# Sinkhorn-sorted attention and a gated MLP on one core: the copies of transposed q and k out of PSUM, with the stride moved from the written side to the read side

## The chip, the core and the metric

The kernel runs on one core of one Trainium2 chip. Its engines are TensorE (PE in the profile; its weight loads are PEld), VectorE (DVE), ScalarE (ACT), GpSimd (POOL) and the queue of SyncE (SP), which only issues DMAs here. Matmul results land in PSUM; DVE and ACT carry them from there to SBUF. The metric is the device time of one execution in microseconds.

## The reference

Four batches of eight heads, 768 tokens, head size 64. The tokens of a head form 8 blocks of 96. A matrix P (8 by 8 for each head, from `sort_net`, five Sinkhorn rounds) mixes the blocks of k and of v; each block of q then attends to the mixed block at its place. The result, 512 wide over all heads, goes through a gated MLP with a mixing over tokens.

```python
P = sort_net
for _ in range(5):
    P = np.exp(P - np.max(P, axis=-1, keepdims=True))
    P = P / (np.sum(P, axis=-1, keepdims=True) + 1e-09)
    P = P / (np.sum(P, axis=-2, keepdims=True) + 1e-09)
k_sorted = np.einsum('bhij,bhjcd->bhicd', P, k_b)     # v_sorted alike
attn = softmax(q_b @ k_sorted^T / sqrt(D))            # in each block of 96
x = (attn @ v_sorted), heads side by side             # 4 x 768 x 512
h = np.maximum(x @ w_in, 0.0)                         # 512 -> 1024
u, v = h[..., :512], h[..., 512:]
v_n = (v - mean(v)) / np.sqrt(var(v) + 1e-06)
v_s = np.einsum('ts,bsd->btd', w_spatial, v_n) + b_spatial[None, :, None]
return (u * v_s) @ w_out
```

## The kernel before

The work is cut into small units, functions whose names begin with `u_`. The order in which they are issued is written out by hand in a table (`ORDER`), one entry for each unit with its arguments; each engine runs its own instructions in that order, one after the other, and waits where an operand or a buffer isn't ready. In the table, batches overlap: while the MLP of one batch runs, the transposes and scores of the next are already issued. A PSUM tile (`ps0` to `ps3`, each two banks of 512 fp32 in all 128 partitions) is named in the entry, and so is the engine that copies it out (A for ACT, D for DVE). `G` is 6, `D` is 64, `n` is 64 or 128.

The loads (`u_L`, on POOL's queue) lay a head's 768 tokens so that partition p holds the tokens 6p to 6p+5: token 6x+g stands in partition x at place g. A transpose with 128 partitions as input thus gives the tokens of one g only, and six of them, one for each g, fill a PSUM tile in the order (g, x).

- `u_QT` transposes q of two heads (`hp`) by matmuls with the identity, g by g, and copies the PSUM tile to `qT` in SBUF, where the tokens stand in their natural order, 6x+g. With `ih` 0 or 1 it does half of the partitions (64, so 384 tokens), with 2 all of them (768 tokens).
- `u_KT` does the same for k, with the mixing matrix `pd` in the identity's place, so that transposing and mixing are one matmul (`mix_T`).
- `u_VM` mixes v in PSUM and copies it to `vm` in SBUF; `u_VC` then copies `vm` to `vb` (one block of 96 tokens in partitions 0 to 95) by eight DMAs for each batch on SP's queue.
- `u_SC` makes the scores of four blocks from `kT` and `qT`, and ACT's exponential writes them to `ex`. `u_AT` multiplies `ex` with `vb`; DVE divides by the sums (`rec`, then `x_sb`).
- `u_SK` is a Sinkhorn round: an exponential on ACT, then sums, reciprocals and products on DVE. The last writes `p_x`, from which `pd` is made. In the table the first four half transposes of q stand between these rounds.
- `u_XT`, `u_VP`, `u_LN`, `u_LA`, `u_UP`, `u_SP` and `u_OP` are the MLP: transposes of x, the two projections, normalisation, spatial mixing with the gate, the output projection and its DMA.

The copies go through one helper, so that in the profile all copies by ACT have line 104 and all by DVE line 106, and the tiles' names tell them apart:

```python
def copy(eng, out, in_):
    if eng == "A":
        nc.scalar.copy(out=out, in_=in_)
    else:
        nc.vector.tensor_copy(out=out, in_=in_)
```

In the profile they are CAST rows, `kT<-ps` and `qT<-ps`. The matmuls of `u_QT` have line 276, of `u_KT` 291, of `u_VM` 313, of `u_SC` 341, of `u_AT` 364, of `u_VP` 405, of `u_UP` 446, of `u_SP` 458, of `u_OP` 479.

Of the kernel before, what the change touches and what calls it, by code (L numbers as in the profile page):

```python
# [59 lines left out]
def kernel(  # L60
# [17 lines left out]
    G = S // 128  # L78
# [20 lines left out]
    def ps_tile(n, dt=FP32):  # L99
        return psum.tile([128, 2, 512 if dt == FP32 else 1024], dt, name=f"ps{n}", tag=f"ps{n}")  # L100
# [6 lines that stand above are left out]
# [153 lines left out]
    def q_tile(b, hp):  # L260
        if ("qT", b, hp) not in st:
            st["qT", b, hp] = att.tile([128, S], BF16, name="qT", tag="qT", bufs=5)
        return st["qT", b, hp]

    def k_tile(b, hp):
        if ("kT", b, hp) not in st:
            st["kT", b, hp] = att.tile([128, S], BF16, name="kT", tag="kT", bufs=5)
        return st["kT", b, hp]

    def u_QT(ps, eng, b, hp, ih):  # L270
        b, hp, ih = int(b), int(hp), int(ih)
        lo, n = (0, 128) if ih == 2 else (ih * 64, 64)
        t = ps_tile(ps).rearrange("p x c -> p (x c)")
        for g in range(G):
            for hh in range(2):
                nc.tensor.matmul(  # L276
                    t[hh * 64:hh * 64 + 64, g * n:(g + 1) * n],
                    lhsT=st["q", b][lo:lo + n, 2 * hp + hh, g * D:(g + 1) * D],
                    rhs=ident[lo:lo + n, lo:lo + n],
                    start=True, stop=True,  # L280
                )
        copy(
            eng,
            q_tile(b, hp)[:, lo * G:(lo + n) * G].rearrange("p (x g) -> p g x", g=G),
            t[:, 0:n * G].rearrange("p (g x) -> p g x", g=G),
        )

    def mix_T(t, src, b, hp, lo, n):
        for g in range(G):
            for hh in range(2):  # L290
                nc.tensor.matmul(  # L291
                    t[hh * 64:hh * 64 + 64, g * n:(g + 1) * n],
                    lhsT=src[:, 2 * hp + hh, g * D:(g + 1) * D],
                    rhs=pd[b][:, 2 * hp + hh, lo:lo + n],
                    start=True, stop=True,
                )

    def u_KT(ps, eng, b, hp, ih):
        b, hp, ih = int(b), int(hp), int(ih)
        lo, n = (0, 128) if ih == 2 else (ih * 64, 64)  # L300
        t = ps_tile(ps).rearrange("p x c -> p (x c)")
        mix_T(t, st["k", b], b, hp, lo, n)
        copy(
            eng,
            k_tile(b, hp)[:, lo * G:(lo + n) * G].rearrange("p (x g) -> p g x", g=G),
            t[:, 0:n * G].rearrange("p (g x) -> p g x", g=G),
        )

    def u_VM(ps, eng, b, hp):
# [217 lines left out]
```

## Time and profile before

| | |
|---|---|
| time, median of 3 runs | 216.38 us (215.75 to 216.55) |
| the profiled execution | 216.17 us, its span 214.0 us |
| busy: PE | 163.0 us (76%) |
| busy: DVE | 133.9 us (63%) |
| busy: ACT | 131.0 us (61%) |
| busy: POOL | 35.3 us (16%) |
| copies of kT and qT on ACT | 13 + 13, 31.8 + 29.4 us |
| copies of kT and qT on DVE | 7 + 7, 12.6 + 15.1 us |
| granted TensorE clock, mean | 0.904 |

Busy time is an average over stages with different limits, so the stages are read apart. The span runs from the first instruction to the last; the execution's time is 2.2 us longer. All times in the rows are microseconds from the span's start, unless they are marked ns. A row of a group has its count behind the x, then the busy time, the mean ns of one, and the engine's idle time just before such instructions with what ended it.

### The profile page before, as it was taken

The numbers are of one execution on the slowest core, as the hardware profiler recorded it, in microseconds if no ns is written. First come the engines' busy times: TensorE is split into PE (matmuls) and PEld (weight loads), VectorE is DVE, ScalarE is ACT, GpSimd is POOL, SyncE is SP. The second block draws the span as 40 slices with busy tenths as digits, with TensorE's granted clock in tenths as the row PEclk, the third lists the DMA queues.
The fourth block names the chain that finished last, engine by engine and source line by source line (L and its number), as shares of the span: only waits on it lengthen the run. The fifth ranks groups of instructions, "written<-read, shape, count | busy, mean of one in ns | idle before, by whom it ended". The sixth has DMA issues, their size and how long they took to land.

```text
span 214.0 us, 4057 instructions
## 1 busy us (share of the span) xinstructions
PE 163.0 (76%) x1716; PEld 101.0 (47%) x1728; DVE 133.9 (63%) x244; ACT 131.0 (61%) x133; POOL 35.3 (16%) x41
## 2 busy tenths in 40 slices
PE   0283856996438969959659996595999999999790
PEld 0241445954335545535424555273665566455330
DVE  3236689776685774524725857589968585664900
ACT  3180854669997699993693769939455524580031
POOL 7405906201300000003430000011000033002000
PEclk9997575599995995888997999999999999999999
DMA  5999999999995000350460042071001600024025
GB/s 93 192 203 206 211 223 236 204 204 204 211 245 93 0 2 3 54 100 0 47 100 3 14 182 101 0 121 35 0 3 39 254 4 0 3 105 189 0 103 193
DMA packets 21921, 22.38 MB, mean 105 GB/s; under 512 B 1040, under 2 KB 18704, under 8 KB 21904
## 3 DMA queue, kind: packets, MB, share of 16 engines
q0 software_dynamic: 14864, 12.19, 36.4%
q1 hardware_dynamic: 7040, 9.94, 16.2%
q8 instruction: 13, 0.21, 0.4%
q14 instruction: 4, 0.03, 0.0%
HBM read 24.78 MB, written 6.29 MB: 145 GB/s over the span
## 4 chain that ended last, share of the span: by engine, by line
PE 53%; ACT 25%; DVE 12%; DMA 5%; issue 3%; POOL 1%; ACTq 0%; DVEq 0%; POOLq 0%
PE ps L458 13%; ACT kT L104 11%; ACT qT L104 10%; PE ps L446 9%; PE ps L405 8%; PE ps L479 8%; DVE qT L106 4%; PE ps L364 4%; DMA q_in<-in_q_dram 4%; PE ps L341 3%; DVE kT L106 3%; PE ps L386 2%; PE ps L313 2%; PE ps L291 2%; ACT u_sb L110 1%
## 5 line engine op out<-in xcount | busy, mean ns | idle before, releaser
L104 ACT CAST kT<-ps 128x768 bf16<-128x768 f32 (+1 forms) x13 | 31.8, 2475 | 9.5 <-PE ps L291 9.5
L458 PE MATMUL ps<-wspT,v_sb 128*128 128x384 bf16 x192 | 34.9, 337 | 3.5 <-ACT kT L104 3.5
L349 ACT ACTIVATE ex<-ps 96x768 bf16<-96x768 f32 x32 | 24.9, 811 | 15.2 <-PE ps L341 15.1
L470 POOL TENSOR_TENSOR gt<-z,u_sb 128x768 bf16<-128x768 f32 x7 | 11.5, 1647 | 129.0 <-DVE z L464 101.1
L104 ACT CAST qT<-ps 128x768 bf16<-128x768 f32 (+1 forms) x13 | 29.4, 2394 | 5.4 <-PE ps L276 5.4
L405 PE MATMUL ps<-w_in_sb,xT 128*128 128x512 bf16 x88 | 24.6, 411 | 4.4 <-ACT kT L104 1.8
L458 PEld LDWEIGHTS <-v_sb 128*128 128x128 bf16 x192 | 18.7, 100 | 16.3 <-issue 5.4
L446 PE MATMUL ps<-xT,w_in_sb 128*128 128x384 bf16 x128 | 24.6, 338 | 0.7 <-ACT kT L104 0.7
L479 PE MATMUL ps<-w_out_sb,gt 128*128 128x512 bf16 x92 | 22.2, 380 | 1.8 <-DVE gt L470 1.7
L464 DVE TENSOR_TENSOR z<-ps,b_bc 128x768 f32<-128x768 f32 x16 | 15.3, 954 | 12.3 <-PE ps L458 12.3
L372 DVE TENSOR_TENSOR x_sb<-ps,rec 96x512 bf16<-96x512 f32 x32 | 22.0, 687 | 1.1
L104 ACT COPY o_sb<-ps 128x1024 f32<-128x1024 f32 x11 | 11.1, 1012 | 17.3 <-PE ps L479 15.9
L419 DVE BATCH_NORM_STATS2 stats<-v_sb 128x6 f32<-128x512 bf16 x24 | 16.3, 677 | 8.7 <-ACT v_sb L110 8.4
L110 ACT ACTIVATE u_sb<-ps 128x768 bf16<-128x768 f32 x16 | 13.0, 810 | 11.1 <-PE ps L446 10.9
L341 PE MATMUL ps<-qT,kT 64*96 64x96 bf16 x256 | 12.1, 232 | 9.1 <-ACT qT L104 4.8
L276 PE MATMUL ps<-ident,q_in 128*64 128x128 bf16 (+1 forms) x240 | 9.4, 233 | 10.8 <-DMA q_in<-in_q_dram 9.2
L364 PE MATMUL ps<-vb,ex 96*128 96x65 bf16 x256 | 14.2, 208 | 3.5 <-ACT qT L104 2.1
L106 DVE CAST qT<-ps 128x768 bf16<-128x768 f32 (+1 forms) x7 | 15.1, 2239 | 2.6 <-PE ps L276 2.6
L446 PEld LDWEIGHTS <-w_in_sb 128*128 128x128 bf16 x128 | 12.3, 100 | 9.2 <-issue 2.0
L341 PEld LDWEIGHTS <-kT 64*96 64x96 bf16 x256 | 9.7, 139 | 14.5 <-issue 12.7
L405 PEld LDWEIGHTS <-xT 128*128 128x128 bf16 x96 | 9.7, 107 | 14.2 <-issue 6.5
L364 PEld LDWEIGHTS <-ex 96*128 96x128 bf16 x256 | 12.7, 107 | 7.3 <-issue 4.2
(63 smaller groups left out, 203.9 us busy)
## 6 DMA issues: line engine op xcount, KB each, us to landing
out_dram<-o_sb SPq DMA_DIRECT2D x12, 512.0 KB, 2.8
vb<-vm SPq DMA_DIRECT2D x32, 99.0 KB, 4.6
v_in<-in_v_dram POOLq DMA_DIRECT2D x4, 768.0 KB, 13.5
k_in<-in_k_dram POOLq DMA_DIRECT2D x4, 768.0 KB, 15.9
q_in<-in_q_dram POOLq DMA_DIRECT2D x3, 768.0 KB, 20.5
wsp_nat<-in_moe_w_spatial_dram POOLq DMA_DIRECT2D x1, 1152.0 KB, 21.9
w_in_sb<-in_moe_w_in_dram POOLq DMA_DIRECT2D x2, 512.0 KB, 16.4
q_in<-in_q_dram POOLq DMA_DIRECT2D x2, 384.0 KB, 10.9
```

Source lines behind the costliest of these rows:

```text
L104: nc.scalar.copy(out=out, in_=in_)
L106: nc.vector.tensor_copy(out=out, in_=in_)
L341: nc.tensor.matmul(t[0:BLK, hh, ii * BLK:(ii + 1) * BLK], lhsT=kT[rows, i * BLK:(i + 1) * BLK], rhs=qT[rows, i * BLK:(i + 1) * BLK], start ...
L349: nc.scalar.activation(out=e[:, 0:2 * NI * BLK].rearrange("p (h c) -> p h c", h=2), in_=t[0:BLK, :, 0:NI * BLK], func=AF.Exp, scale=scale,)
L364: nc.tensor.matmul(t[:, hh, ii * VW:ii * VW + D + 1], lhsT=e[:, c:c + 128], rhs=vb[b % 2][:, ih * NI + ii, 2 * hp + hh, 0:D + 1], start=Tr ...
L372: nc.vector.tensor_mul(out=x_sb[:, :, hp * 128:hp * 128 + 128].rearrange("p i (h d) -> p h i d", h=2), in0=tv[:, :, :, 0:D], in1=_raw_ap(r ...
L405: nc.tensor.matmul(t[:, x, :], lhsT=st["xT", b][:, kc, n * 128:(n + 1) * 128], rhs=w_in_sb[:, kc, DH:DFF], start=(kc == 0), stop=(kc == KC ...
L419: nc.vector.bn_stats(out=stats, in_=v_sb[:, x, :])
L446: nc.tensor.matmul(t[:, x, 0:HW], lhsT=w_in_sb[:, kc, mc * 128:(mc + 1) * 128], rhs=st["xT", b][:, kc, ih * HW:(ih + 1) * HW], start=(kc = ...
L458: nc.tensor.matmul(t[:, x, 0:HW], lhsT=st["v_sb", b, n][:, mc * 128:(mc + 1) * 128], rhs=wspT[:, n, x * HW:(x + 1) * HW], start=(n == 0), ...
L464: nc.vector.tensor_add(out=z.rearrange("p (x c) -> p x c", x=2), in0=t[:, :, 0:HW], in1=b_bc.rearrange("p (x c) -> p x c", x=2),)
L479: nc.tensor.matmul(t[:, x, :], lhsT=st["gt", b, mc][:, c * 128:(c + 1) * 128], rhs=w_out_sb[:, mc, :], start=(mc == 0), stop=(mc == FC - 1),)
```

## The change

The copy's loops are put in another order. Before, it ran over g outside and x inside: PSUM was read one element after the other, and `qT` or `kT` was written with a step of G elements. Now it runs over x outside and g inside: the 384 or 768 elements in SBUF are written one after the other, and PSUM is read with a step of `n` fp32, six times, then from the next x. What is moved and where it ends up is the same. All instructions, their order on each engine and the DMAs are the same.

```diff
@@ u_QT
         copy(
             eng,
-            q_tile(b, hp)[:, lo * G:(lo + n) * G].rearrange("p (x g) -> p g x", g=G),
-            t[:, 0:n * G].rearrange("p (g x) -> p g x", g=G),
+            q_tile(b, hp)[:, lo * G:(lo + n) * G].rearrange("p (x g) -> p x g", g=G),
+            t[:, 0:n * G].rearrange("p (g x) -> p x g", g=G),
         )
@@ u_KT
         copy(
             eng,
-            k_tile(b, hp)[:, lo * G:(lo + n) * G].rearrange("p (x g) -> p g x", g=G),
-            t[:, 0:n * G].rearrange("p (g x) -> p g x", g=G),
+            k_tile(b, hp)[:, lo * G:(lo + n) * G].rearrange("p (x g) -> p x g", g=G),
+            t[:, 0:n * G].rearrange("p (g x) -> p x g", g=G),
         )
```

## The prediction

> **What bounds the kernel now.** I read the page's chain first, to see which engine the end hangs on, then the busy times by stage, then who TensorE (PE) waited for, and last the rows of the copies.
>
> ```profile
> PE 53%; ACT 25%; DVE 12%; DMA 5%; issue 3%; POOL 1%; ACTq 0%; DVEq 0%; POOLq 0%
> PE ps L458 13%; ACT kT L104 11%; ACT qT L104 10%; PE ps L446 9%; PE ps L405 8%; PE ps L479 8%; DVE qT L106 4%; PE ps L364 4%; DMA q_in<-in_q_dram 4%; PE ps L341 3%; DVE kT L106 3%; PE ps L386 2%; PE ps L313 2%; PE ps L291 2%; ACT u_sb L110 1%
> ```
>
> Over half of the chain is PE. The copies that the change touches (kT and qT, on ACT and DVE) are 11 + 10 + 4 + 3 = 28% of it, 60 of 214 us. That isn't what can be won: shortened, they hand the chain to PE. So the question is how long PE is idle, stage by stage (columns: length, PE busy, weight load, DVE, ACT, POOL, granted clock, DMA share, GB/s):
>
> ```profile
> 0.00:20.00 20.00, 7.54 (x76) 4.34 (x76) 7.62 (x38) 7.42 (x10) 8.34 (x17) 0.98 1.09 171
> 20.00:40.00 20.00, 14.10 (x250) 11.05 (x248) 16.93 (x23) 12.14 (x13) 11.61 (x14) 0.59 1.24 220
> 40.00:65.00 25.00, 16.91 (x246) 12.75 (x246) 18.23 (x26) 21.43 (x17) 2.92 (x3) 0.91 1.29 215
> 65.00:160.00 95.00, 77.94 (x816) 47.26 (x822) 60.78 (x106) 69.28 (x67) 7.47 (x5) 0.90 0.23 47
> 160.00:200.00 40.00, 39.84 (x307) 22.75 (x309) 27.00 (x52) 17.66 (x25) 4.93 (x3) 1.00 0.21 79
> 200.00:214.00 14.00, 6.71 (x32) 2.81 (x31) 3.32 (x4) 3.04 (x3) 0.00 (x0) 0.99 0.30 113
> ```
>
> PE is idle for 5.9 us in 20 to 40, 8.1 in 40 to 65 and 17.1 in 65 to 160. From 160 to 200 it is never idle, and in the last 14 us stands the tail of the last batch; no copy of q or k lies there, so nothing is to be won after 160. In 20 to 65 the DMA share is above 1, so what lands there lands late. The list of PE's waits in 65 to 160 has ten rows that name such a copy, from the first here to the last, 16.2 of the 17.1 us together:
>
> ```profile
> PE ps L458 <- ACT kT L104: 3.5, 2, 1.8
> PE ps L341 <- ACT kT L104: 2.3, 2, 1.8
> PE ps L341 <- ACT qT L104: 2.2, 1, 2.2
> ...
> PE ps L341 <- DVE qT L106: 0.2, 1, 0.2
> ```
>
> No single wait is over 2.2 us, so they are of the size of one copy: a PSUM tile or a kT/qT that comes free one copy too late.
>
> **The change, part by part.** Nothing is added, removed or moved: the same instructions stand in the same order on every engine, and the DMAs are the same. Each of the 40 copies now writes its 384 or 768 bf16 one after the other and reads PSUM with a step of 64 or 128 fp32 (256 or 512 bytes); before, it read one after the other and wrote with a step of 6 bf16 (12 bytes). So there are two prices: the strided write that goes and the strided read that comes. Groups by shape, mean ns last before the idle time:
>
> ```profile
> L104 ACT CAST kT<-ps 128x768 bf16<-128x768 f32 x10 | 27.5, 2786 | 4.4 <-PE ps L291 4.4
> L104 ACT CAST qT<-ps 128x768 bf16<-128x768 f32 x8 | 22.5, 2915 | 0.0
> L104 ACT CAST qT<-ps 128x384 bf16<-128x384 f32 x5 | 6.8, 1561 | 5.4 <-PE ps L276 5.4
> L106 DVE CAST qT<-ps 128x768 bf16<-128x768 f32 x4 | 10.5, 2775 | 2.0 <-PE ps L276 2.0
> L104 ACT CAST vm<-ps 128x768 bf16<-128x768 f32 x12 | 10.5, 893 | 0.8 <-PE ps L313 0.8
> L106 DVE CAST vm<-ps 128x768 bf16<-128x768 f32 x4 | 3.8, 958 | 3.0 <-PE ps L313 2.8 <-issue 0.2
> L110 ACT ACTIVATE v_sb<-ps 128x512 bf16<-128x512 f32 x2 | 1.2, 597 | 1.5 <-PE ps L405 1.4
> ```
>
> The vm copies move as many elements, of the same types, out of the same PSUM, in runs of 64 on both sides, in a third of the time, on either engine. The rows of the strided copies overlap a little; their pace is seen where two stand back to back, 2.64 us each:
>
> ```profile
> 54.01 5.28 ACT L104 CAST kT<-ps 128x768 bf16<-128x768 f32 x2
> ```
>
> With a read that costs nothing extra a full copy would take 0.89 us and give back 1.75; a half would take about 0.5 (an estimate: from 512 elements to the vm row's 768 the time grows by 1.16 ns each, which leaves 449 ns at 384; rounded up) and give back 0.8. What a strided PSUM read costs, no row shows at this size. The nearest four, all on DVE:
>
> ```profile
> L371 DVE RECIPROCAL rec<-ps 96x8 f32<-96x8 f32 x32 | 6.4, 199 | 10.5 <-PE ps L364 10.4
> L195 DVE TENSOR_REDUCE colsum<-p_all 32x8 f32<-32x64 f32 x5 | 1.3, 254 | 0.2
> L192 DVE TENSOR_REDUCE rowsum<-p_all 32x8 f32<-32x64 f32 x5 | 1.0, 203 | 7.6 <-ACT p_all L191 7.6
> L193 DVE RECIPROCAL rowsum<-rowsum 32x8 f32<-32x8 f32 x5 | 1.0, 191 | 0.2
> ```
>
> The reciprocal of rec reads 8 elements from PSUM at a step of 66 fp32, four in each of two banks; that of rowsum reads 8 neighbours from SBUF. The difference is 8 ns, at most 1.0 ns an element even if the place of the data costs nothing. The two reductions read the same 64 elements of SBUF, colsum with a step of 8 fp32: 51 ns more, 0.8 ns an element. So the lower bound is 0 extra (0.89 us a full copy), and by the colsum row it is 0.61 us (1.5 us). An upper bound from rows there is none: eight elements are few, and ACT has no strided read at all; the worst that a row shows for any stride is the present write, 3.4 ns an element (2.64 us / 768). I take 0 extra, since the rec row is the only one that reads PSUM, and keep 1.5 us and 2.64 us as rivals.
>
> The Trainium skill speaks against the change: "SBUF — State Buffer", section "Door 1: The DMA port swizzle (why `[64,N]` ≈ `[32,N]`)", gives SBUF lines of 16 bytes with steps up to 8 bf16 free, and PSUM lines of 8 bytes, where it says non-contiguous patterns slow matmuls. By that the present write, 6 bf16, should be free and the new read, hundreds of bytes a step, should pay: no gain in the sum, and the loss of the last rival below. The first half does not agree with this trace (2.64 us against 0.89); the second half no run here shows yet.
>
> Now the sum, stage by stage.
>
> *Start.* Four half copies of q stand on ACT between the exponentials (p_all) of the Sinkhorn loop, and p_x is its last step:
>
> ```profile
> 9.78 1.44 ACT L104 CAST qT<-ps 128x384 bf16<-128x384 f32 x1 [4.46 <-PE ps L276]
> 10.85 0.42 ACT L191 ACTIVATE p_all<-p_all 32x64 f32<-32x64 f32 x1
> 11.06 4.09 ACT L104 CAST qT<-ps 128x384 bf16<-128x384 f32 x3
> 14.73 0.42 ACT L191 ACTIVATE p_all<-p_all 32x64 f32<-32x64 f32 x1
> 16.68 0.26 ACT L191 ACTIVATE p_all<-p_all 32x64 f32<-32x64 f32 x1 [1.52 <-DVE p_all L205]
> 18.24 1.54 POOL L199 TENSOR_TENSOR p_x<-p_all,colsum 32x512 bf16<-32x512 f32 x1 [10.54 <-DVE colsum L196]
> ```
>
> With halves of 0.5 us the first exponential ends near 10.55; DVE's 1.53 us of loop (15.15 to 16.68) then ends at 12.1, after the three other halves (12.0), so the second runs to 12.35, the third to 14.15, and p_x starts at 15.5 in place of 18.24: 2.7 us. PE's dummy matmuls there lie beside it.
>
> *20 to 65.* PE's waits on copies shrink, but next late is vb, which SP's queue copies out of vm and the AT matmuls (L364) read. Four issues for batch 0's first half, then four for batch 1's, each with its time to landing, and the first AT of each batch:
>
> ```profile
> L328 SPq DMA_DIRECT2D vb<-vm x4: 581/625/710, 25.5 to 27.5; - x4
> DMA to landing us min/median/max: 5.4/5.7/5.9
> L328 SPq DMA_DIRECT2D vb<-vm x4: 572/595/612, 54.1 to 56.0; - x4
> DMA to landing us min/median/max: 5.6/5.9/6.4
> 35.46 0.60 PE L364 MATMUL ps<-vb,ex 96*128 96x65 bf16 x8 [0.72 <-DVE kT L106]
> 65.71 0.62 PE L364 MATMUL ps<-vb,ex 96*128 96x65 bf16 x8
> 53.02 1.01 ACT L104 CAST vm<-ps 128x768 bf16<-128x768 f32 x1
> ```
>
> Batch 0's vb lands near 27.5 + 5.8 = 33.3, so beyond the start's 2.7 us its AT can come at most 2.2 earlier: I take 2.2 of the 5.9 idle. Batch 1's lands near 62; its last vm copy stands on ACT behind a full kT copy, and comes 1.75 earlier, so vb lands near 60.3 and the AT of 65.71 gains 5.4 at most, out of 8.1 idle. I take it.
>
> *65 to 160.* A full copy gives back 1.75, the waits are up to 2.2: I take 14 of the 16.2, and 2 stay for waits a little longer than a copy or for what ACT does next (the exponentials ex).
>
> *The clock.* In four stretches behind such waits the granted clock is half; the same 8 matmuls of L446 take 2.75 us in one and 1.46 outside. Their sum, PE first:
>
> ```profile
> sum 20.40, PE 17.75 PEld 10.18 DVE 10.04 ACT 15.20 POOL 0.11; mean PE 4.44 PEld 2.54 DVE 2.51 ACT 3.80 POOL 0.03
> ...
> 84.75 2.75 PE L446 MATMUL ps<-xT,w_in_sb 128*128 128x384 bf16 x8
> 142.04 1.46 PE L446 MATMUL ps<-xT,w_in_sb 128*128 128x384 bf16 x8
> ```
>
> All warm, 17.75 x 0.47 = 8.3 us would go; none, if the clock falls anyway. I take 5, since one of the four lies where PE will wait for vb. "TensorE: Matmul & The Clock Gate" of the Trainium skill, section "What's actually happening", lets the clock fall after an idle window of about 3.4 us; here it fell behind shorter waits that follow one another, so rule and trace agree only in part. By the rule alone waits this short would leave PE warm, 8.3 would stand in place of 5, and the sum would give 184.
>
> Sum: 2.7 + 2.2 + 5.4 + 14 + 5 = 29.3 us. The profiled execution took 216.17 us around its span of 214.0, near the runs' median of 216.38. 216.17 - 29.3 = 187 us.
>
> **Rivals.** *Half rate:* the read costs what colsum's does, a full copy 1.5 us, a half 0.8. For it: eight elements show little. The start gains 1.6, 20 to 65 still some 6.5 (vb binds), 65 to 160 ten (16.2 us in waits of some 2 us are eight, each shortened by 1.1, and the small ones go), the clock 4: 22 us, 194. *Read as dear as the write:* the stride's cost moves sides, copies stay at 2.64 us, 216. Against it: rec's at most 1.0 ns extra an element. For it: both engines, of unequal pace elsewhere, lie at the same pace here, so it is a memory that sets it, and PSUM may be no better. *Slower:* a PSUM read at such a step is dearer than 3.4 ns an element; at 5 ns, say, each full copy takes 1.2 us more, and the waits of some 2 us grow by it, about eight in 65 to 160 and, by the idle time, six before: 17 us, 233. It decides from 3.4 ns on, and the rec row speaks against it. The Trainium skill's page "SBUF — State Buffer", in the section named above, speaks for it.
>
> **How the numbers follow.** No extra cost 0.50, half rate 0.35, as dear as now 0.07, dearer 0.08. The likeliest gives 187, by itself 181 (16.2 waits, 8.3 clock) to 192 (no clock gain). With half rate and no clock gain the time is 198, so 180 to 199 holds both, 0.8 with what may be mis-sized in them. Faster by over 0.5%, about what a measurement here tells from none, 0.85; within it 0.07; slower 0.08.
>
> **What would show it.** Right: rows of kT and qT at 0.9 us (ACT) and 1.0 (DVE) for 768, p_x near 15.5, PE idle under 3 us in what is now 65 to 160, AT of batch 1 waiting for a vb DMA, ACT's share of the chain near nothing, no change after 160. Rows of 1.5 us are the second case, of 2.6 the third. Wrong: rows as forecast and yet PE idle, for then another wait took their place.

## The result and the profile after

The changed kernel took 182.97 us (median of 4 runs, 180.44 to 184.14) against 216.47 before: a ratio of 0.8385, 95% interval 0.828 to 0.849. Two of the four runs were slow ones, and the ratio is that of the other two (182.69 and 180.44) to the runs before; the two medians alone would give 0.845. Run again later it took 183.43 (6 runs, 181.20 to 184.02), ratio 0.845 (0.840 to 0.850). The forecast was 187. All rows of "after" below are from the profile of that second set, whose execution took 183.53 us with a span of 181.4; its rows agree with the first set's.

The chain of work that ended last, by the page of this profile: the copies of kT and qT are gone from it, PE has gone from 53% to 68%, and a DMA that was not in its first fifteen lines, `vb<-vm`, with its issue on SP's queue, holds 11%.

```profile
PE 68%; DMA 13%; DVE 6%; ACT 4%; SPq 4%; issue 2%; POOL 1%; ACTq 0%; DVEq 0%; POOLq 0%
PE ps L458 15%; PE ps L405 12%; PE ps L446 12%; PE ps L479 9%; DMA vb<-vm 7%; PE ps L364 5%; SPq L328 4%; DMA q_in<-in_q_dram 4%; PE ps L341 4%; PE ps L386 3%; PE ps L313 3%; PE ps L276 2%; PE ps L291 2%; DVE z L464 2%; DVE gt L470 2%
```

The groups of copies by shape, each with its mean in ns ahead of the idle time. By their means, copies of 768 on ACT have gone from 2786 and 2915 ns to 802 and 804, on DVE from 2775 to 949, and are as quick as the vm copies, which read PSUM in runs of 64: reading PSUM with a step of 128 fp32 costs nothing extra that these rows show.

```profile
L104 ACT CAST vm<-ps 128x768 bf16<-128x768 f32 x12 | 9.3, 803 | 2.4 <-PE ps L313 2.4
L104 ACT CAST kT<-ps 128x768 bf16<-128x768 f32 x10 | 7.9, 802 | 3.7 <-PE ps L291 3.7
L104 ACT CAST qT<-ps 128x768 bf16<-128x768 f32 x8 | 6.2, 804 | 0.5 <-PE ps L276 0.4
L106 DVE CAST vm<-ps 128x768 bf16<-128x768 f32 x4 | 3.7, 952 | 0.2 <-issue 0.2
L106 DVE CAST qT<-ps 128x768 bf16<-128x768 f32 x4 | 3.6, 949 | 0.0
...
L104 ACT CAST qT<-ps 128x384 bf16<-128x384 f32 x5 | 2.2, 468 | 9.8 <-PE ps L276 9.8
```

What PE waited for: us in total, how often, and the longest wait. Before, the rows that name kT or qT held 28.8 us over the whole span; now there is none, and vb stands in their place:

```profile
PE ps L364 <- DMA vb<-vm: 9.0, 9, 2.0
PE ps L276 <- DMA q_in<-in_q_dram: 8.4, 1, 8.4
PE ps L479 <- DVE gt L470: 1.7, 2, 1.5
```

To see where the 32.6 us of span went, I take four points that both traces have. First ACT's rows at the start:

```profile
8.99 0.48 ACT L104 CAST qT<-ps 128x384 bf16<-128x384 f32 x1 [3.67 <-PE ps L276]
9.37 0.25 ACT L191 ACTIVATE p_all<-p_all 32x64 f32<-32x64 f32 x1
9.52 1.19 ACT L104 CAST qT<-ps 128x384 bf16<-128x384 f32 x3
11.12 0.26 ACT L191 ACTIVATE p_all<-p_all 32x64 f32<-32x64 f32 x1 [0.41 <-DVE p_all L205]
12.88 0.26 ACT L191 ACTIVATE p_all<-p_all 32x64 f32<-32x64 f32 x1 [1.50 <-DVE p_all L205]
14.44 1.54 POOL L199 TENSOR_TENSOR p_x<-p_all,colsum 32x512 bf16<-32x512 f32 x1 [6.75 <-DVE colsum L196]
```

The first copy starts 0.8 us earlier than in the profile before (9.78); that is the landing of the first q, for which PE waited 8.4 us here, 9.2 before and 9.0 in the first set's profile. p_x starts at 14.4 in place of 18.24, 5.4 us after the first copy in place of 8.5: 3.0 us from the change. Second, batch 1's first AT (L364) and the projection behind it (L405). The first row is that projection before, the others are after:

```profile
66.14 0.62 PE L405 MATMUL ps<-w_in_sb,xT 128*128 128x512 bf16 x1
...
53.17 0.19 PE L364 MATMUL ps<-vb,ex 96*128 96x65 bf16 x1 [1.36 <-DMA vb<-vm]
53.85 0.19 PE L364 MATMUL ps<-vb,ex 96*128 96x65 bf16 x1 [0.49 <-DMA vb<-vm]
54.54 0.19 PE L364 MATMUL ps<-vb,ex 96*128 96x65 bf16 x1 [0.50 <-DMA vb<-vm]
55.31 0.31 PE L364 MATMUL ps<-vb,ex 96*128 96x65 bf16 x5 [0.57 <-DMA vb<-vm]
55.45 1.43 PE L405 MATMUL ps<-w_in_sb,xT 128*128 128x512 bf16 x3
```

At the start of the projection (66.14 and 55.45) 10.7 us are won, 6.9 of them since p_x. Third, from there to the last matmul of the scores, which starts at 165.9 before and 133.2 now. The stretch of before and then of after (length, PE busy, PEld, DVE, ACT, POOL, clock, DMA share, GB/s):

```profile
66.14:165.90 99.76, 82.87 (x870) 49.52 (x875) 65.16 (x114) 71.42 (x71) 7.47 (x5) 0.91 0.21 44
```

```profile
55.45:133.20 77.75, 76.57 (x871) 46.79 (x876) 59.94 (x114) 47.32 (x70) 7.47 (x5) 0.96 0.45 86
```

Here 22.0 us are won: PE's idle time fell from 16.9 to 1.2 (15.7 us), and the busy time of the same matmuls (870 and 871 records) by 6.3, with the granted clock up from 0.91 to 0.96. Fourth, from there to the end: 48.1 before, 48.2 now. So 0.8 + 3.0 + 6.9 + 22.0 + 0 = 32.7, which is the whole of it but for rounding.

### The profile page after: what moved, and what is told of

Same layout as the page of the kernel before. It is cut to its first block, busy times and chain, and to the rows that moved or that the text cites. A ratio compares the mean times of both kernels' runs of the same rounds, so it can differ in the third digit from the quotient of the medians.

```text
span 182.0 us, 4057 instructions
## 1 busy us (share of the span) xinstructions
PE 154.3 (85%) x1716; PEld 95.9 (53%) x1728; DVE 117.2 (64%) x244; ACT 90.7 (50%) x133; POOL 35.2 (19%) x41
## 4 chain that ended last, share of the span: by engine, by line
PE 68%; DMA 13%; DVE 6%; ACT 4%; SPq 4%; issue 2%; POOL 1%; ACTq 0%; DVEq 0%; POOLq 0%
PE ps L458 15%; PE ps L405 12%; PE ps L446 12%; PE ps L479 9%; DMA vb<-vm 8%; PE ps L364 5%; DMA q_in<-in_q_dram 4%; SPq L328 4%; PE ps L341 4%; PE ps L386 3%; PE ps L313 3%; PE ps L276 2%; PE ps L291 2%; DVE z L464 2%; DVE gt L470 2%
## 5 line engine op out<-in xcount | busy, mean ns | idle before, releaser
L458 PE MATMUL ps<-wspT,v_sb 128*128 128x384 bf16 x192 | 33.2, 326 | 0.0
L405 PE MATMUL ps<-w_in_sb,xT 128*128 128x512 bf16 x88 | 25.0, 417 | 0.6 <-issue 0.2
L458 PEld LDWEIGHTS <-v_sb 128*128 128x128 bf16 x192 | 18.1, 98 | 11.5
L446 PE MATMUL ps<-xT,w_in_sb 128*128 128x384 bf16 x128 | 23.3, 326 | 0.0
L364 PE MATMUL ps<-vb,ex 96*128 96x65 bf16 x256 | 14.9, 203 | 8.6 <-DMA vb<-vm 8.6
L104 ACT COPY o_sb<-ps 128x1024 f32<-128x1024 f32 x11 | 11.1, 1012 | 17.3 <-PE ps L479 15.9
L364 PEld LDWEIGHTS <-ex 96*128 96x128 bf16 x256 | 12.4, 104 | 12.7 <-issue 6.4
L371 DVE RECIPROCAL rec<-ps 96x8 f32<-96x8 f32 x32 | 6.3, 197 | 15.9 <-PE ps L364 15.6
L276 PE MATMUL ps<-ident,q_in 128*64 128x128 bf16 (+1 forms) x240 | 8.4, 221 | 9.0 <-DMA q_in<-in_q_dram 9.0
L479 PEld LDWEIGHTS <-gt 128*128 128x128 bf16 x96 | 8.8, 97 | 11.9 <-DVE gt L470 2.3
L405 PEld LDWEIGHTS <-xT 128*128 128x128 bf16 x96 | 9.4, 106 | 10.6 <-issue 2.9
L104 ACT CAST qT<-ps 128x768 bf16<-128x768 f32 (+1 forms) x13 | 8.4, 675 | 10.5 <-PE ps L276 10.4
L104 ACT CAST kT<-ps 128x768 bf16<-128x768 f32 (+1 forms) x13 | 9.4, 727 | 8.2 <-PE ps L291 8.2
L276 PEld LDWEIGHTS <-q_in 128*64 128x64 bf16 (+1 forms) x240 | 6.9, 120 | 9.5 <-DMA q_in<-in_q_dram 9.0
## 6 DMA issues: line engine op xcount, KB each, us to landing
q_in<-in_q_dram POOLq DMA_DIRECT2D x2, 384.0 KB, 10.7
```

The lines of the kernel that those rows point to most:

```text
L276: nc.tensor.matmul(t[hh * 64:hh * 64 + 64, g * n:(g + 1) * n], lhsT=st["q", b][lo:lo + n, 2 * hp + hh, g * D:(g + 1) * D], rhs=ident[lo:lo ...
L364: nc.tensor.matmul(t[:, hh, ii * VW:ii * VW + D + 1], lhsT=e[:, c:c + 128], rhs=vb[b % 2][:, ih * NI + ii, 2 * hp + hh, 0:D + 1], start=Tr ...
L405: nc.tensor.matmul(t[:, x, :], lhsT=st["xT", b][:, kc, n * 128:(n + 1) * 128], rhs=w_in_sb[:, kc, DH:DFF], start=(kc == 0), stop=(kc == KC ...
L446: nc.tensor.matmul(t[:, x, 0:HW], lhsT=w_in_sb[:, kc, mc * 128:(mc + 1) * 128], rhs=st["xT", b][:, kc, ih * HW:(ih + 1) * HW], start=(kc = ...
L458: nc.tensor.matmul(t[:, x, 0:HW], lhsT=st["v_sb", b, n][:, mc * 128:(mc + 1) * 128], rhs=wspT[:, n, x * HW:(x + 1) * HW], start=(n == 0), ...
L479: nc.tensor.matmul(t[:, x, :], lhsT=st["gt", b, mc][:, c * 128:(c + 1) * 128], rhs=w_out_sb[:, mc, :], start=(mc == 0), stop=(mc == FC - 1),)
```

## The experiments

The theory after the result: a written step is dear, a read step in PSUM is free, and the copies made PE wait in groups. Its rivals are that the write is dear for some other reason (the loop's shape, the place), that each copy simply gave back its own time, and that a copy of a length between the two would do nearly as well.

### What a stride costs

Copies of 384 elements added behind the changed kernel's work, each line four times, on ACT and on DVE (the first lines as they stand, the rest left out):

```diff
+        [nc.scalar.copy(out=wbA[:, 0:2304].rearrange("p (n s) -> p n s", s=6)[:, :, 0], in_=f4[:, 0:384]) for _ in range(4)]
+        [nc.scalar.copy(out=wbA[:, 0:384], in_=f4[:, 0:384].rearrange("p (g x) -> p x g", g=6)) for _ in range(4)]
+        ...
```

> The changed kernel, with copies of 384 elements added at its end, first on ACT and then on DVE, four of each kind, one after the other: from PSUM fp32 to bf16 with written steps of 1, 2, 3, 4, 6 and 8 elements, pairs every 12, to fp32 with steps of 1, 2, 3, 4 and 6, from PSUM with a read step of 2 and of 64, and from SBUF bf16 with a step of 6 read or written. Theory: reading PSUM with a step is free (0.47 us on ACT and 0.55 on DVE, as contiguous), and a written step of 6 bf16 costs 1.3 to 1.4 us on both engines. For what makes the write dear there are three rivals. Width: a lone 2-byte element is dear at any step, from 2 on 1.3 us or more, and fp32 at a step is cheap (0.5). Distance: it goes by bytes, so 6 bf16 costs what 3 fp32 costs, and 2 bf16 is cheap. Lines of 16 bytes, free up to 8 bf16 and 4 fp32: all but 6 fp32 at 0.5 us, which the rows of kT before already speak against.

By line (L506 to L511: bf16 written with a step of 1, 2, 3, 4, 6, 8; L512: pairs of bf16 every 12; L513 to L517: fp32 with 1, 2, 3, 4, 6; L518 and L519: PSUM read with 2 and 64, written contiguously; L531: DVE, bf16 with 6; L540: DVE, PSUM read with 64), min, median and max in ns:

```profile
L506 ACT CAST wsp_nat<-ps x4: 478/478/478, 177.7 to 179.2; 128x384 bf16<-128x384 f32 x4
L507 ACT CAST wsp_nat<-ps x4: 584/584/585, 179.8 to 181.6; 128x384 bf16<-128x384 f32 x4
L509 ACT CAST wsp_nat<-ps x4: 1007/1007/1007, 185.5 to 188.6; 128x384 bf16<-128x384 f32 x4
L510 ACT CAST wsp_nat<-ps x4: 1431/1431/1432, 189.7 to 194.1; 128x384 bf16<-128x384 f32 x4
L511 ACT CAST wsp_nat<-ps x4: 1855/1855/1855, 195.5 to 201.2; 128x384 bf16<-128x384 f32 x4
L512 ACT CAST wsp_nat<-ps x4: 493/493/493, 203.1 to 204.6; 128x384 bf16<-128x384 f32 x4
L516 ACT COPY wsp_nat<-ps x4: 830/831/831, 212.1 to 214.7; 128x384 f32<-128x384 f32 x4
L517 ACT COPY wsp_nat<-ps x4: 826/826/827, 215.5 to 218.1; 128x384 f32<-128x384 f32 x4
L518 ACT CAST wsp_nat<-ps x4: 478/478/478, 219.0 to 220.5; 128x384 bf16<-128x384 f32 x4
L519 ACT CAST wsp_nat<-ps x4: 478/478/478, 221.0 to 222.5; 128x384 bf16<-128x384 f32 x4
L531 DVE CAST wspT<-ps x4: 1430/1430/1431, 236.5 to 240.9; 128x384 bf16<-128x384 f32 x4
L540 DVE CAST wspT<-ps x4: 557/557/557, 269.1 to 270.8; 128x384 bf16<-128x384 f32 x4
```

Reading PSUM with a step of 2 or 64 costs to the nanosecond what reading it in order costs. Writing costs by distance: from step 2 to 8 the bf16 rows on ACT lie on 160 ns + 0.552 ns x step x 384 (step 6: 1432, measured 1431), so an element pays 0.55 ns for every 2-byte place that the write moves on; at step 1 the line would give 372, and the copy takes 478. fp32 grows evenly too, by 0.44 ns an element for every 4-byte place (495, 662 and 831 at steps 2 to 4), and then stays (826 at 6). The pairs cost 493 ns for as many elements, a third of the lone ones with the same mean step. So none of the three rivals holds whole. It is not width alone, since step 2 is cheap. It does not go by bytes, since 12 bytes a step cost 1431 ns in bf16 and 662 in fp32. And steps within 16 bytes are not free: 16 bytes is where the price stops growing, at least for fp32.

A second set, of 256 elements and three of each, asked where it ends for bf16, and why DVE wrote a step of 6 from SBUF in 0.80 us and not 1.43.

```diff
+        [nc.scalar.copy(out=wbA[:, 0:4096].rearrange("p (n s) -> p n s", s=16)[:, :, 0], in_=fA[:, 0:256]) for _ in range(3)]
+        [nc.vector.tensor_copy(out=wbD[:, 0:1536].rearrange("p (n s) -> p n s", s=6)[:, :, 0], in_=srcf[:, 0:256]) for _ in range(3)]
+        ...
```

> The changed kernel with copies of 256 elements added at its end, three of each kind, first on ACT and then on DVE: from PSUM to bf16 with written steps of 1, 6, 7, 8, 9, 12 and 16, from SBUF fp32 with 1 and 6, from SBUF bf16 with 1, 2, 4, 6, 8 and 16. The run before gave 0.55 ns for each 2-byte place that a written bf16 steps over, up to 8 places, on both engines. Theory (the cost is for 16 bytes at most, as fp32 was flat from step 4 on): 9, 12 and 16 cost what 8 does, 4.4 ns an element, 1.3 us. Rival (it walks on): 12 costs 6.6 ns, 1.85 us, and 16 costs 8.8 ns, 2.4 us. For DVE's step of 6 from SBUF, which cost 0.80 us for 384 in place of 1.43: if it is the source's place, fp32 from SBUF is as cheap (1.7 ns an element, 0.5 us); if it is bf16 to bf16, fp32 costs 3.3 ns, 1.0 us.

ACT from PSUM with 8 (L507), 12 (L509) and 16 (L510); ACT from SBUF fp32 with 6 (L512); DVE with 6 from PSUM (L525), from SBUF fp32 (L532) and from SBUF bf16 (L536):

```profile
L507 ACT CAST wsp_nat<-ps x3: 1289/1290/1290, 184.7 to 187.3; 128x256 bf16<-128x256 f32 x3
L509 ACT CAST wsp_nat<-ps x3: 1278/1278/1279, 192.6 to 195.2; 128x256 bf16<-128x256 f32 x3
L510 ACT CAST wsp_nat<-ps x3: 1226/1227/1227, 196.5 to 199.0; 128x256 bf16<-128x256 f32 x3
L512 ACT CAST wsp_nat<-w_in_sb x3: 1041/1042/1042, 201.6 to 203.7; 128x256 bf16<-128x256 f32 x3
L525 DVE CAST wspT<-ps x3: 1006/1007/1008, 202.7 to 204.8; 128x256 bf16<-128x256 f32 x3
L532 DVE CAST wspT<-w_in_sb x3: 592/593/593, 226.0 to 227.3; 128x256 bf16<-128x256 f32 x3
L536 DVE COPY wspT<-w_in_sb x3: 593/593/594, 231.2 to 232.5; 128x256 bf16<-128x256 bf16 x3
```

From 8 places (16 bytes) on the price, beyond the 160 ns, stays at 4.2 to 4.4 ns an element: it stops growing, as fp32's did. DVE writes the same step in 593 ns in place of 1007 when it reads SBUF, fp32 or bf16, and each place then costs it 0.27 ns (732 ns at step 8, 311 at 2) in place of 0.55. ACT gains nothing from it (1042). So the price is not the written memory's alone; why DVE is quicker from SBUF the runs don't say.

### Half of the copies

Only kT's copies turned round, or only qT's (the change in one of the two functions):

> Only the copies of kT are turned round; those of qT write with a step as before. Theory (PE waits for copies that stand in groups on ACT, k and q mixed, and a shorter member of a group shortens the wait of the whole): more than half of the 33.5 us is won by one half of the copies, about 20 us, so 196. Rival (each copy gives back its own time): kT's rows hold 44.4 of the 88.9 us that the copies took, so half, 200. Second rival (a wait ends with its last copy, whichever was long): a third or less, 205 or more.

> Only the copies of qT are turned round. Theory of groups: about 20 us won, of them 2.7 at the start (four half copies of q between the Sinkhorn rounds), 196; the gains of this and of the kT run add up to more than 33.5. Rival of own times: 200, and the two gains add up to 33.5. Second rival (last copy decides): 205 or more.

kT alone: 193.67 us (ratio 0.891, 0.883 to 0.898), 23.1 won. qT alone: 194.83 (0.898, 0.893 to 0.903), 21.9 won. Together that is 45 us for a whole of 33.5, more than the whole, as the theory of groups had forecast. But PE's waits show another reason for it. Of the 28.8 us before, 18.1 name kT and 10.7 qT. With kT alone turned round 11.6 still name qT, and with qT alone 17.0 still name kT. So each half took away about its own waits, and a shorter neighbour in a group hardly shortened the other's. What is won twice is mostly PE's busy time, here from the pages of before, kT alone, qT alone and both:

```profile
PE 163.0 (76%) x1716; PEld 101.0 (47%) x1728; DVE 133.9 (63%) x244; ACT 131.0 (61%) x133; POOL 35.3 (16%) x41
PE 155.5 (81%) x1716; PEld 96.9 (50%) x1728; DVE 126.1 (65%) x244; ACT 109.5 (57%) x133; POOL 35.3 (18%) x41
PE 154.9 (80%) x1716; PEld 97.1 (50%) x1728; DVE 125.0 (65%) x244; ACT 111.7 (58%) x133; POOL 35.3 (18%) x41
PE 154.1 (85%) x1716; PEld 95.8 (53%) x1728; DVE 117.2 (65%) x244; ACT 90.7 (50%) x133; POOL 35.3 (19%) x41
```

Either half alone brings the same 1716 matmuls down by some 8 us (7.5 and 8.1), and both together by only 8.9: that is 6.7 us counted twice. The clock goes with it: with kT alone turned round the granted clock is 1.00 from 75 to 145 us, though 7.6 of PE's 14.1 us of idle time there remain (before: 0.90). The spans fell by 21.3, 21.0 and 32.6 us, so 9.7 are counted twice in all; the other 3.0 lie in PE's idle time, where vb's waits are 9.0 us with both halves and only 3.1 and 1.5 with one. Why half of the waits leave the clock up is not shown.

Only ACT's copies:

```diff
-            q_tile(b, hp)[:, lo * G:(lo + n) * G].rearrange("p (x g) -> p x g", g=G),
+            q_tile(b, hp)[:, lo * G:(lo + n) * G].rearrange("p (x g) -> p x g" if eng == "A" else "p (x g) -> p g x", g=G),
```

(and alike for the PSUM side and for kT)

> Only the copies on ACT (26 of 40) are turned round; the 14 on DVE write with a step as before. Theory: DVE's copies bind in 20 to 40 us (some 4.6 us of PE waits there) and in the pair of qT at 60 to 65 us, and hardly after: 5 to 8 us are lost against the whole change, 188 to 191. Rival (share of the copies' time, 27.7 of 88.9 us on DVE): 10 us lost, 193. Rival that DVE's copies are hidden: 183.

185.98 us (0.859, 0.855 to 0.863): some 3 us behind the whole change, less than the 5 to 8 expected, though DVE's copies then stand in 11.1 us of PE's waits. The waits for vb, 9.0 us in the changed kernel, have gone from this run's list: a wait on a copy that is taken away is partly followed by one for vb, and so is not all won.

### A copy at half rate

```diff
-        copy(
-            eng,
+        for _ in range(2):
+            copy(
+                eng,
```

(and alike for kT)

> The change, and each copy of kT and qT done twice in the new form, so that a full one takes some 1.6 us: the half-rate case, which the chip does not have by itself. By the sum of the half-rate case: 194 (about a third of the gain lost). Rival (time runs in a straight line with the copy's length, 0.80 us at 183 and 2.64 at 216.5): 198. Rival (PE's own work hides a copy up to some 1.6 us): 184 to 187.

191.51 us (0.882, 0.877 to 0.887). With copies of 1.6 us, 11.8 us of PE's waits name them, against 28.8 at 2.6 us and none at 0.8. The half-rate rival had 194, the straight line 198: a quarter of the gain is lost for 43% of the copy's saving (0.80 us of 1.84). Had the read cost as much as colsum's, the time would still have been inside the forecast's range: that the range held says little on the price of the read.

### The next thing late: vb

The changed kernel without the loads of q, k and v of batches 1 to 3 (batch 0's tiles stand in for them):

```diff
         src = {"q": q, "k": k, "v": v}[x]
+        if b > 0:
+            st[x, b] = st[x, 0]
+            return
```

> The changed kernel without the loads of q, k and v for batches 1 to 3, which use batch 0's tiles instead; the weights are loaded as before. Theory: PE's 8.6 us of waits for vb come from vb's DMAs sharing 16 busy engines with the loads, so batch 1's waits (3.6 us) go, vb lands in some 2.8 us there, the half clock behind them (some 2.5 us of PE time) goes too, and batch 0's 5.0 us shrink a little: 175 to 178. Rival: what is late is the issue on SP's queue, 0.6 us each and eight in a row; then the waits stay at 2 us or more for batch 1 and the time at 180 to 183. Rival: the loads slow PE or the copies elsewhere too; then under 174.

177.96 us (0.825, 0.819 to 0.831), at the upper end of the theory's 175 to 178. Batch 1's vb: first the landing of its last DMA without the later loads, then its first four issues in the changed kernel:

```profile
52.72 2.71 DMA vb<-vm
```

```profile
L328 SPq DMA_DIRECT2D vb<-vm x4: 572/596/597, 47.4 to 49.3; - x4
DMA to landing us min/median/max: 5.7/5.8/6.0
```

Alone, vb lands in 2.7 us, beside the loads in 5.8. PE's waits for batch 1's vb fall from 3.5 to 1.4 us (0.41 + 0.48 + 0.46; the issues of 0.6 us one after the other remain), and the half clock behind them is gone. Batch 0's waits stay at 5.5: there the loads of batch 0 and of the weights keep the DMA share at 1.17 (20 to 33 us).

Moving one load, w_out, to a later place was not enough:

```diff
-... XT:1:D:0:0:1 L:wo SC:2:0:0:1 ...
+... L:k:3:0:128 L:wo KT:0:A:2:3:2 ...
```

> The changed kernel with the load of w_out moved behind the last load of k on POOL's queue, from batch 0's to batch 3's place; it is read first by the output projection some 40 us later. Theory (loads and vb share the DMA engines): batch 2's loads end some 5 us earlier, so batch 1's second half of vb meets less traffic, its waits fall by about 1 us, 181 to 183. Rival: the engines stay full until batch 2's loads are in, nothing to be measured, 183. Rival: the later load meets batch 2's or 3's vb or starves the output projection, 184 or more.

183.06 us (0.846, 0.842 to 0.850), the same; waits for vb 8.1 us. This is what the rival said that the DMA engines stay full until batch 2's loads are in, and from 50 to 60 us their share is 1.26 with and without the move.

Making vb ready earlier (three places of the order table), beside the changed kernel on the same chip:

```diff
-KT:1:A:0:2:0 L:v:1:0:128 VM:2:D:0:3 VM:3:A:0:0 VM:1:D:0:2 VM:0:A:0:1 KT:2:A:0:0:0 QT:3:D:0:1:1 KT:1:D:0:1:0 KT:0:D:0:3:0
+L:v:1:0:128 VM:2:D:0:3 VM:3:A:0:0 VM:1:D:0:2 VM:0:A:0:1 KT:2:A:0:2:0 QT:3:D:0:1:1 KT:1:D:0:1:0 KT:0:D:0:3:0 KT:2:A:0:0:0
-AT:1:0:2:0 PD:1:0:4 QT:2:A:0:0:1
+QT:2:A:0:0:1 AT:1:0:2:0 PD:1:0:4
-KT:1:A:1:2:2 XT:2:D:0:1:1 VM:3:A:1:3
+VM:1:A:1:3 XT:2:D:0:1:1 KT:3:A:1:2:2
```

> The changed kernel with three places of the order table changed, so that vb is ready earlier where PE now waits for it: in batch 0 the first half of kT comes behind the four mixings of v in place of ahead of them, and one half transpose of q comes ahead of the first AT; in batch 1 the last mixing of v changes place with a transpose of k. Theory (vb is the next late thing after the change): its DMAs are issued 0.4 us earlier in batch 0 and 0.7 in batch 1, and 0.4 us of q's work fall into the wait: 1 to 1.5 us less than the changed kernel beside it, 181 to 182, and up to 2.5 more where the half clock ends a window earlier. Rival (vb's landing is set by the loads, whenever it is issued): the same as the changed kernel, 182 to 184.

> The changed kernel once more, on the same chip as its rearranged version beside it. 182 to 184 us.

181.88 us (6 runs, 180.69 to 183.24; ratio 0.840, 0.836 to 0.845) against 183.43 (181.20 to 184.02; 0.845, 0.840 to 0.850): 1.5 us less in the median, as expected in size, but the two intervals overlap, so it is not shown to be faster than the change alone. PE's waits for vb fell from 9.0 to 4.6 us, but other waits came in their place (for p_x, kT and ex among them): PE's idle time as a whole is 27.2 us, against 27.3. In batch 1 the earlier issue is lost again: the DMAs were issued at 46.7 in place of 47.4 and took 6.5 us in place of 5.8.

```profile
L328 SPq DMA_DIRECT2D vb<-vm x4: 571/596/602, 46.7 to 48.6; - x4
DMA to landing us min/median/max: 6.5/6.5/6.7
```

### The half clock that is left

By the trace's record of the clock, two stretches at half clock remain in the changed kernel, 13.7 us from about 25 on and 6.8 from about 56 on, at batch 0's and batch 1's waits for vb. Dummy matmuls, put where PE waits:

```diff
-AT:1:0:2:0
+DM:1:14:384 AT:1:0:2:0
-AT:2:1:2:0
+DM:2:18:384 AT:2:1:2:0
```

> The changed kernel with dummy matmuls (384 columns of zeros, their result is not used) where PE now waits for vb: 14 ahead of batch 0's first AT, 18 ahead of batch 1's. Theory (the half clock in the 13.7 and 6.8 us behind these waits comes from PE standing idle there): batch 1's half-clock stretch goes, worth some 2.5 us of PE time, and batch 0's ends up to two windows of 3.4 us earlier, worth 1 to 2: 179 to 180. Rival (the clock falls for another cause, batch 0's for the thin matmuls of kT, qT and scores before it): the stretches stay, 183 to 184. Rival (the dummies run past the landing of vb): 185 or more.

183.93 us (0.847, 0.842 to 0.852): no gain over the changed kernel's 0.845. Yet the clock did what the theory said. The stretch of 20 to 40 us, first in the changed kernel, then with the dummies (PE's busy time has them in it):

```profile
20.00:40.00 20.00, 14.08 (x253) 11.17 (x254) 10.01 (x22) 8.08 (x12) 7.81 (x9) 0.66 1.24 220
```

```profile
20.00:40.00 20.00, 16.72 (x243) 12.35 (x238) 10.74 (x23) 9.10 (x14) 6.94 (x7) 0.83 1.24 220
```

The granted clock there rose from 0.66 to 0.83, the half-clock stretches shrank to 6.8 and 3.4 us, and the time did not follow. The DMA engines are as full as before, and PE, now quicker, comes to batch 1's second half of vb too early (a wait of 1.52 us, where it was 0.56). Since taking the later loads away did shorten the kernel, I read this as a kernel that its DMAs bind up to some 60 us, where a faster PE is worth little; that every us of the clock was lost to vb is not shown.

Both together, with 8 dummies in batch 0:

> The rearranged order of before (v mixed first) with the same dummies, 8 in batch 0 and 18 in batch 1. Theory: the two add up as far as each shortens its own thing, 178 to 179. Rival that the dummies do nothing: 182.

182.21 us in the median (6 runs, 178.34 to 182.95). The run of 178.34 had a mean clock of 0.982, the others, from 181.44 on, 0.946 to 0.963. No interval is on record for so uneven a set, and the median is near that of the rearranged order alone (181.88). This is inconclusive: that it is a better version is not shown.

## Why the prediction was right

- *The price of the read* was taken from the smallest of rows, eight elements at 1.0 ns extra at most, and from that 0 was chosen, which the row allowed and did not show. It came right: 0.80 us a full copy on ACT, 0.95 on DVE, 0.47 and 0.55 a half (0.89 and 0.5 were put in). The argument for the third rival, that both engines go at one pace and so a memory sets it, was half true: from SBUF DVE goes at nearly twice that pace (593 ns in place of 1007).
- *Start:* 2.7 predicted, 3.0 measured from the first copy.
- *20 to 65:* 2.2 + 5.4 = 7.6 predicted, 6.9 measured. The step "next late is vb" was right, in the place named. By its sum vb should let batch 1's AT go at 55.4 (65.71 - 10.3); the last of its first four waits ended at 55.31, 0.8 us of that by the earlier first landing. What it didn't see is that AT's matmuls wait block by block, so that the first starts when one DMA has landed, and the last waits for the fourth.
- *65 to 160:* 14 predicted, 15.7 measured. I had left 2 us for waits a little longer than a copy, and nothing of them stayed. Where a copy's own saving falls short, its neighbour's helps: 0.3 us of the scores' waits (L341) still name ACT's qT with qT alone turned round, and nothing with both.
- *The clock:* 5 predicted, a choice between 0 and 8.3, and 6.3 measured in the same stretch. Of the four stretches at half clock behind the copies one remains, the first, where PE waits for vb, as supposed. The whole 8.3 would have given 184, nearer to the measured time, but not for its reason: the clock still fell to half behind vb's waits, none of them over 2.0 us.
- *After 160* nothing, as said (48.1 and 48.2).
- The sum came to 29.3 and the span fell by 32.6, 0.8 of it by an earlier first landing. So the mechanism held at each of these steps, and the two terms of the long middle stretch, 19 for 22.0, were sized too low.

The Trainium skill's page "SBUF — State Buffer" ("Door 1: The DMA port swizzle (why `[64,N]` ≈ `[32,N]`)") would have given the wrong sign. Its 16 bytes show up in these runs, as the distance at which a strided write stops getting dearer (1290 ns at 8 places, 1278 at 12), not up to which it is free. Its statement on PSUM is on matmuls, which no run here tries with a step; for reads by ACT and DVE a step of 64 cost nothing. On the Trainium skill's page "TensorE: Matmul & The Clock Gate" ("What's actually happening") the rule that PE idle brings the clock down agrees with the dummy matmuls (0.66 to 0.83). The time did not follow (183.93 us).

## What to carry to other kernels

When a copy out of PSUM has to change the order of its elements, let it read with the step and write one after the other: on ACT and DVE the strided read out of PSUM was free here, and a lone bf16 written 12 bytes further each time cost 3.3 ns. What a shorter copy is worth is not its own time but PE's waits behind it: add those up, count what the clock gives back only once (here half of the copies brought most of it), and look for the DMA that is late next. Where PE waits for a DMA soon after, a higher granted clock may be worth nothing, as I read the run with the dummy matmuls.

## What the runs showed of the hardware that I had not expected

- The price of a written step grows evenly: 0.55 ns for each 2-byte place, on ACT and on DVE alike from PSUM, to 16 bytes and no further (384 bf16 on ACT: 584 ns at step 2, 1431 at 6, 1855 at 8; 256 bf16: 1290 at 8, 1278 at 12).
- Two neighbouring bf16 cost hardly more than one: 493 ns in pairs every 12 places, against 1431 singly every 6.
- DVE reading SBUF writes the same step in 593 ns where it takes 1007 from PSUM; ACT takes 1042 and 1008. Why is not shown.
- The same DMA of vb takes 2.7 us alone and 5.4 to 7.7 beside loads that fill the engines, and issued 0.7 us earlier it landed no earlier (46.7 + 6.5 and 47.4 + 5.8 us).
- Either half of the copies turned round brings the busy time of the same 1716 matmuls down by 7.5 or 8.1 us, both together by 8.9.
